# Three attention pairs a cycle instead of two, and a reordered seam inside batch 0, in a fused attention and ReLU-squared kernel

## The chip, the cores and the metric

The program runs on one core of a Trainium2 chip. The metric is device time in microseconds (us) of one execution; lower is better. PE is TensorE, ACT is ScalarE, DVE is VectorE, POOL is GpSimd and SP is SyncE. L286 means line 286 of the kernel before the change.

## The reference

Attention over 8 batches, 12 heads, 448 positions and 64 head dimensions, with one extra term in the softmax denominator, then a two-layer block whose activation is the square of a ReLU:

```
scores = q @ k^T / 8
attn   = exp(scores) / (sum(exp(scores)) + 1)          (written with the maximum taken out)
x      = (attn @ v), heads side by side: 3584 tokens x 768
h      = x @ w_in        (768 x 2048)
out    = relu(h)^2 @ w_out   (2048 x 768), float32
```

Inputs and output are float32; the kernel multiplies in 16 bits and sums in 32.

## The kernel before, in words

**Units.** The work is cut into 54 units in `units`: (batch, pair of heads, first query, number of queries). Batch 0 is done in two query parts, of 192 queries (units 0 to 5) and of 256 (units 6 to 11). From batch 1 on (units 12 to 53) a unit is a pair of heads with all 448 queries. Keys are taken in 4 groups of 112 (`RUN` is 4).

**A unit's steps.** `begin` takes its tiles: `et` for the exponentials (pool of 4), `es` and `half` for their sums. `scores(u, et, c)` (L178) makes half of its scores, c = 0 or 1: two key groups, each in its own PSUM tile `sp`, of which there are two, and ACT takes the exponential of each into `et` (L169). So the second half can only be written where ACT has emptied the first. `add_chunks` (L209) sums the four key groups on DVE in three additions (steps 0, 1, 2; for the short units of batch 0 two, steps 1 and 2), `row_sums` (L239) sums over partitions on PE (L250) and takes the reciprocal on ACT as Ln and Exp (L253, L254): this is Z. `values` (L232) is the product with v on PE (L236), and `normalise` (L257) multiplies by 1/Z on DVE into `xt` (L262 for one unit, L265 for two short ones).

**The two products behind it.** `tile_in` (L290) multiplies xt by w_in, one block of 128 hidden features at a time (two for short parts): 6 steps of two matmuls for a block of 448 tokens, each step half the array wide (L286); DVE then takes the ReLU (L303) and squares it into `gs` (L305). `tile_out` (L320) multiplies gs by w_out for 128 tokens and one half of the 768 columns, in 16 steps. These tasks stand as generators in the lists `ins` and `outs`; `drain(ns)` takes first-product steps up to an amount of time, `run(tiles, n)` whole tasks, `rows(n)` n steps of the second product.

**Modes of PE.** Everything is tiled over halves of PE's array. Scores and `rows` use 64 rows by 128 columns (`ROWS2`: two matmuls side by side into two PSUM tiles, L332, which DVE and ACT add up at L339, L341 and L343). The values, the sums, the transposes and the first product use 128 rows by 64 columns (`COLS2`). At the end, and in `keep_warm` (L427, a product of zeros), the whole array is one piece.

**PSUM.** Two `sp` tiles of two banks each, one bank `xp` and three banks `mp`. From unit 18 on `mp_tile` uses the four single banks in turn.

**Order.** The order is written out by hand, and each engine runs its instructions in that order. Units 0 to 5 (L465) and 6 to 11 (L497) interleave scores, values, transposes of batch 1 and, from unit 7 on, `drain` of the first product for the first 192 tokens. Units 12 to 17 (L536) do the same for batch 1 and drain the rest of that product and the one of the next 256 tokens. Batches 0 to 2 get q and k transposed by PE (`transposes`, L151, at the units of `transpose_at`, L419), later ones by DMA on SP's queue from copies in memory (`stage`, `transposed_loads`). Then 18 cycles (L586) of two units each, three cycles to a batch:

```
scores a, rows(11), scores a, rows(11), scores b, rows(10), scores b      (the stretch in row mode)
values and normalise of the two units before (pending); additions of b    (column mode from here)
pr == 0: rest of ins, queue the first product of batch b-1, one tile_out, loads for batch b+1
early tasks of ins; row_sums of a and b; the other tasks of ins
```

A batch has 16 tasks of `tile_in`, spread 3, 7 and 6 over its three cycles, and 7 halves of `tile_out` on average. After the loop come the last values, three tasks of `tile_out`, and the products of batch 7.

**Loads.** POOL's queue carries, in order, v, the 16-bit q and k of batches 0 to 2 (`load_natural`, tiles `qn` and `kn` in pool `nat`), w_in, w_out and the copies for later batches. A load into a `nat` tile waits until the transposes that read its former contents are done.

Of the kernel before, what the change touches and what calls it, by code (L numbers as in the profile page):

```python
# [15 lines left out]
def kernel(  # L16
# [33 lines left out]
    qk_pool = ctx.enter_context(tc.tile_pool(name="qk", bufs=2))  # L50
    e_pool = ctx.enter_context(tc.tile_pool(name="e", bufs=4))
    es_pool = ctx.enter_context(tc.tile_pool(name="es", bufs=2))
    z_pool = ctx.enter_context(tc.tile_pool(name="z", bufs=2))
    r_pool = ctx.enter_context(tc.tile_pool(name="r", bufs=2))
    osb_pool = ctx.enter_context(tc.tile_pool(name="osb", bufs=2))

# [26 lines left out]
    def load_natural(b, p0, p1):  # L83

        raw = b == 0 and p1 <= 3
        for n, r in (("q", q_r), ("k", k_r)):
            src = r[b, :, 2 * p0:2 * p1]
            if raw:
                if p0 == 0:
                    whole[n] = e_pool.tile([P, RUN * S], FP32, name="et")  # L90
                t = whole[n][:, p0 * 512:(p0 + 1) * 512].rearrange("p (h t d) -> p h t d", h=2, t=RUN)
                (nc.sync if n == "q" else nc.scalar).dma_start(out=t, in_=src)
            else:
                if p0 % 3 == 0:
                    whole[n] = nat.tile([P, NPAIR, RUN, D], FP16, name=f"{n}n{p0 // 3}")
                t = whole[n][:, 2 * (p0 % 3):2 * (p0 % 3 + p1 - p0)]
# [223 lines left out]
    def tile_out(tok, n0, w):  # L320

        if n0 == 0:
            ots[tok] = osb_pool.tile([128, DM], FP32, name="ot")
        ot = ots[tok]
        rows = mode[0] == ROWS2
        op = mp_tile()
        lo = mp_tile() if rows else None
        for fb in range(NFFB):
            g = gs[:, fb, tok % RING:tok % RING + 128]
            if rows:  # L330
                for x, o in ((0, op), (64, lo)):
                    nc.tensor.matmul(o[:, 0:w], g[x:x + 64], wout[x:x + 64, fb, n0:n0 + w],  # L332
                                     start=(fb == 0), stop=(fb == NFFB - 1))
            else:
                product(op[:, 0:w], g, wout[:, fb, n0:n0 + w], start=(fb == 0), stop=(fb == NFFB - 1))
            if fb < NFFB - 1:
                yield w / 2.4
        if rows and n0 == 0:
            nc.vector.tensor_scalar(out=ot[:, n0:n0 + w], in0=op[:, 0:w], scalar1=OUT_SCALE, scalar2=None, op0=ALU.mult)  # L339
        else:  # L340
            nc.scalar.activation(out=ot[:, n0:n0 + w], in_=op[:, 0:w], func=AF.Copy, scale=OUT_SCALE)  # L341
# [52 lines left out]
    def left():  # L394
        return sum(t[0] for t in ins)
# [20 lines left out]
    units += [(b, pr, 0, S) for b in range(1, B) for pr in range(NPAIR)]  # L416
    NU = len(units)

    transpose_at = {pr - 1: (0, pr) for pr in range(1, NPAIR)}  # L419
    for pr in range(NPAIR):  # L420
        transpose_at[NPAIR + 3 + pr] = (1, pr)
    transpose_at[16], transpose_at[17] = (2, 0), (2, 1)

    def keep_warm(n):
        wp = m_psum.tile([128, 512], FP32, name="mp")
# [11 lines left out]
        nc.gpsimd.tensor_copy(last_of, qks[b][0:1, :, 0:1])  # L437

    def begin(i):
        ets[i] = e_pool.tile([P, RUN * 2 * S], FP16, name="et")  # L440
        es = es_pool.tile([P, 2 * S], FP16, name=f"es{i % 2}")
        half = es_pool.tile([P, 1024], FP16, name="half")
        ess[i] = (es, half)
        return units[i], ets[i], es, half
# [20 lines left out]
    for i in range(NPAIR):  # L465
        u, et, es, half = begin(i)
        mode[0] = COLS2
        scores(u, et, 0)
        if i < 2:
            scores(u, et, 1)  # L470
        if i in (3, 5):
            rcp = sums_of(i - 3)
        if i == 0:
            transposes(0, 1, lambda: cast(0, 2, "q"))
            cast(0, 2, "k")
        elif i in transpose_at:
            transposes(*transpose_at[i])
        if i == 0:
            keep_warm(1)
        if i:  # L480
            sums(i - 1)
        if i == 4:
            xp = x_psum.tile([128, 512], FP32, name="xp")
            values_of(2, xp)
        if i > 1:
            scores(u, et, 1)
        if i == 2:
            xp = x_psum.tile([128, 512], FP32, name="xp")
        if i in (2, 3, 4):
            values_of(i - 2 if i < 4 else 3, xp)  # L490
        if i in (3, 5):
            normalise(units[i - 3:i - 1], xp, rcp)
        if i in (1, 3, 5):
            keep_warm(1 + i // 5)


    for i in range(NPAIR, 2 * NPAIR):  # L497
# [4 lines left out]
        mode[0] = COLS2  # L502
        scores(u, et, 0)
        if i == NPAIR:
            values_of(i - 2, xp)
            sums(i - 1)
        if i in transpose_at:
            transposes(*transpose_at[i])
        if i > NPAIR:
            drain(share[0] * 0.45)  # L510
        scores(u, et, 1)
        values_of(i - 1, xp)
        if i == NPAIR:
            keep_warm(2)
        if two:
            rcp = sums_of(i - 2)
        if i > NPAIR:
            drain(share[0] * 0.3)
        else:
            keep_warm(2)  # L520
            normalise(two, xp, rcp)
            queue(0, FIRST)
            share[0] = left() / (NPAIR + 2)
        add_chunks(u, et, es, half, 1)
        if two and i > NPAIR:
            normalise(two, xp, rcp)
# [2 lines left out]
            drain(share[0] * 0.25)  # L529
        if i == NPAIR + 5:  # L530
            load_natural(2, 0, 3)
            for j in range(2):
                load_wout(0, j, 2)


    for i in range(2 * NPAIR, 3 * NPAIR):  # L536
# [4 lines left out]
            xp = x_psum.tile([128, 512], FP32, name="xp")  # L541
        mode[0] = COLS2
        scores(u, et, 0)
        if i in transpose_at:
            transposes(*transpose_at[i])
        if i == 2 * NPAIR + 2:
            load_natural(2, 3, 6)
            for j in range(2):
                load_wout(HALF, j, 2)
            load_v(2, 0, 6)  # L550
            stage(3)
        drain(left() * 0.5 if first else share[0] * 0.45)
        scores(u, et, 1)
        if first:
            done = units[i - 2:i]
# [7 lines left out]
        for step in range(3):  # L563
            add_chunks(u, et, es, half, step)
            drain(share[0] * (0.15, 0.1, 0.15)[step])
        if i == 3 * NPAIR - 1 and ins and ins[0][0] < ins[0][1]:
            run(ins)
        normalise(done, xp, rcp)
        if first:
            queue(FIRST, S - FIRST)  # L570
            share[0] = left() / (NPAIR + 1.5)

# [10 lines left out]
            n -= 1  # L583
        mode[0] = COLS2

    for c in range((NU - 3 * NPAIR) // 2):  # L586
        i = 3 * NPAIR + 2 * c
        b, pr = units[i][0:2]
        new = []
        for j in range(2):  # L590
            new.append(begin(i + j))
        (ua, ea, sa, ha), (ub, eb, sb, hb) = new
        scores(ua, ea, 0)
        rows(11)
        scores(ua, ea, 1)
        add_chunks(ua, ea, sa, ha, 0)
        rows(11)
        scores(ub, eb, 0)
        add_chunks(ua, ea, sa, ha, 1)
        add_chunks(ua, ea, sa, ha, 2)  # L600
        rows(10)
        scores(ub, eb, 1)
        add_chunks(ub, eb, sb, hb, 0)
        mode[0] = COLS2
        for at in pending:
            if at not in rcps:
                rcps[at] = row_sums([units[at]], (ess.pop(at)[0:1],))
            xp = mp_tile()
            values(units[at], ets.pop(at), xp)
            normalise([units[at]], xp, rcps.pop(at))  # L610
        add_chunks(ub, eb, sb, hb, 1)
        add_chunks(ub, eb, sb, hb, 2)
        if b in ON_PE and pr + 2 < NPAIR:
            transposes(b, pr + 2)
            transposes(b, pr + 3)
# [12 lines left out]
        n, early = ((3, 0 if b > 2 else 1), (7, 3), (6, 3))[pr // 2]  # L628
        run(ins, early)
        for at in (i, i + 1):  # L630
            rcps[at] = row_sums([units[at]], (ess.pop(at)[0:1],))
        run(ins, n - early)
        if pr == NPAIR - 2:
            complete(b * S)
        pending = [i, i + 1]
    for at in pending:
        xp = mp_tile()
        values(units[at], ets.pop(at), xp)
        normalise([units[at]], xp, rcps.pop(at))
    mode[0] = FULL  # L640
    run(outs, 3)
    queue((B - 1) * S, S)
# [31 lines left out]
```

## Time and profile before

| | us |
|---|---|
| median of 3 runs | 417.7 (417.44 to 418.12) |
| the profiled execution, its own time | 417.37 |
| its span, first to last instruction | 415.60 |
| PE busy, share of the span | 405.1, 97% |
| DVE busy | 278.0, 67% |
| ACT busy | 238.9, 57% |
| scores of unit 6 / 12 / 18 / 24 begin at | 17.88 / 37.16 / 67.08 / 116.26 |
| one batch of the cycles (batch 4) | 163.75 to 211.25 |

"Busy" counts a matmul from its start to its modelled end, and matmuls overlap, so a busy PE need not be at its peak: whether time is lost is seen from the distances between starts. A timeline line gives start, length, engine, line, operation, result<-inputs, shape and count of merged instructions, and in brackets the idle time before with what ended it. The clock row gives the granted PE clock in tenths; it is full throughout.

### The profile page before, as it was taken

Reading aid. Unit: us, or ns where it says so; the run is one execution under the profiler, and the core shown is the slowest. Engines: PE = TensorE matmul, PEld = TensorE weight load, DVE = VectorE, ACT = ScalarE, POOL = GpSimd, SP = SyncE. Lnnn points to the kernel's source line nnn. Section 1 sums busy time; section 2 is a strip of 40 time slices with the busy share of each in tenths; the row PEclk is TensorE's granted clock in tenths of the full one; section 3 lists DMA queues with packets and bytes.
Section 4 is the critical chain, followed back from the end, with each engine's and each line's share of the span. In section 5 each row is a group of like instructions: output and inputs, shape, how many; then the busy total and the mean of one; then the engine's idle time right before and its main releaser. Section 6 shows DMA issues by size and latency. Waiting matters only on the chain.

```text
span 415.6 us, 10692 instructions
## 1 busy us (share of the span) xinstructions
PE 405.1 (97%) x4719; PEld 256.0 (62%) x4719; DVE 278.0 (67%) x535; ACT 238.9 (57%) x330; POOL 36.4 (9%) x58
## 2 busy tenths in 40 slices
PE   7899999899999999999999999999999999999997
PEld 3567666566566666665666666665666666555664
DVE  4769888778865868568766769659676669287000
ACT  5987998674675664673575564673766655100111
POOL 7523310020000200002000300001000000000000
PEclk9999999999999999999999999999999999999999
DMA  9999999879109960199509871198101101010222
GB/s 202 197 197 198 201 201 219 153 117 207 40 2 196 182 140 2 49 194 185 130 2 171 156 157 35 39 190 151 45 2 39 39 2 39 39 39 0 77 76 77
DMA packets 75823, 45.58 MB, mean 110 GB/s; under 512 B 42560, under 2 KB 72000, under 8 KB 75456
## 3 DMA queue, kind: packets, MB, share of 16 engines
q0 software_dynamic: 28848, 22.16, 35.0%
q1 hardware_dynamic: 46208, 22.05, 23.2%
q8 instruction: 37, 0.61, 0.6%
q10 hardware_dynamic: 720, 0.69, 0.6%
q14 instruction: 10, 0.08, 0.1%
HBM read 45.69 MB, written 17.93 MB: 153 GB/s over the span
## 4 chain that ended last, share of the span: by engine, by line
PE 86%; DMA 8%; ACT 2%; DVE 2%; issue 1%; POOL 0%; POOLq 0%
PE mp L286 23%; PE mp L332 17%; PE mp L288 11%; PE xp L286 8%; PE sp L201 6%; PE xp L332 6%; PE mp L236 5%; DMA kn<-in_k_dram 4%; PE xp L288 3%; DMA win<-in_moe_w_in_dram 3%; PE xp L236 3%; PE sp L189 2%; DMA vn<-in_v_dram 2%; PE mp L250 2%; ACT et L169 1%
## 5 line engine op out<-in xcount | busy, mean ns | idle before, releaser
L169 ACT ACTIVATE et<-sp 112x896 f16<-112x896 f32 (+2 forms) x192 | 165.8, 914 | 53.9 <-PE sp L201 40.2
L286 PEld LDWEIGHTS <-win 128*64 128x64 f16 x1536 | 85.3, 110 | 45.3 <-issue 2.5
L286 PE MATMUL mp<-xt,win 128*64 128x448 f16 (+2 forms) x1236 | 110.2, 324 | 1.2 <-DVE xt L265 0.5
L332 PE MATMUL mp<-wout,gs 64*128 64x384 f16 x864 | 102.3, 322 | 0.0
L332 PEld LDWEIGHTS <-gs 64*128 64x128 f16 x1152 | 56.1, 94 | 31.8
L303 DVE TENSOR_SCALAR rt<-mp 128x448 f16<-128x448 f32 (+2 forms) x99 | 61.5, 621 | 17.2 <-PE mp L286 13.2
L305 DVE TENSOR_TENSOR gs<-rt 128x448 f16<-128x448 f16 (+2 forms) x128 | 50.2, 392 | 4.4
L332 PE MATMUL xp<-wout,gs 64*128 64x384 f16 x288 | 52.6, 323 | 0.0
L253 ACT ACTIVATE rcp<-mp,one_b 128x448 f32<-128x448 f32 (+2 forms) x40 | 25.2, 629 | 40.2 <-PE mp L250 35.9
L214 DVE TENSOR_TENSOR es<-et 112x896 f16<-112x896 f16 x42 | 26.1, 620 | 17.7 <-ACT et L169 17.6
L341 ACT ACTIVATE ot<-mp 128x384 f32<-128x384 f32 (+1 forms) x29 | 14.1, 487 | 36.2 <-PE mp L288 27.6
L201 PE MATMUL sp<-qk 64*112 64x224 f16 x480 | 33.8, 260 | 0.0
L288 PEld LDWEIGHTS <-gs 128*128 128x128 f16 x256 | 24.4, 98 | 15.1 <-issue 0.4
L286 PE MATMUL xp<-xt,win 128*64 128x448 f16 x300 | 32.6, 352 | 0.0
L201 PEld LDWEIGHTS <-qk 64*112 64x112 f16 x480 | 26.3, 128 | 9.7 <-issue 5.4
L236 PEld LDWEIGHTS <-vn 112*64 112x64 f16 x432 | 22.0, 109 | 15.5 <-issue 4.6
L288 PE MATMUL mp<-wout,gs 128*128 128x384 f16 (+1 forms) x192 | 31.0, 322 | 0.0
L343 DVE SCALAR_TENSOR_TENSOR ot<-mp,ot 128x384 f32<-128x384 f32 x27 | 15.1, 558 | 21.7 <-PE sp L201 11.5
L254 ACT ACTIVATE rcp<-rcp 128x448 f32<-128x448 f32 (+2 forms) x48 | 27.7, 577 | 1.5
L216 DVE TENSOR_TENSOR es<-es,half 112x896 f16<-112x896 f16 x42 | 26.2, 625 | 1.4
L189 PE MATMUL sp<-qk 64*112 64x448 f16 (+2 forms) x192 | 24.3, 322 | 2.1 <-ACT et L169 1.3
L214 DVE TENSOR_TENSOR half<-et 112x896 f16<-112x896 f16 x42 | 25.9, 616 | 0.3 <-ACT et L169 0.3
(61 smaller groups left out, 306.6 us busy)
## 6 DMA issues: line engine op xcount, KB each, us to landing
vn<-in_v_dram POOLq DMA_DIRECT2D x7, 672.0 KB, 8.0
out_dram<-ot SPq DMA_DIRECT2D x9, 384.0 KB, 2.3
win<-in_moe_w_in_dram POOLq DMA_DIRECT2D x8, 384.0 KB, 14.0
wout<-in_moe_w_out_dram POOLq DMA_DIRECT2D x4, 768.0 KB, 12.8
stage_q<-in_q_dram POOLq DMA_DIRECT2D x4, 676.0 KB, 10.5
stage_k<-in_k_dram POOLq DMA_DIRECT2D x4, 676.0 KB, 13.6
out_dram<-ot SPq DMA_DIRECT2D x8, 288.0 KB, 2.9
out_dram<-ot SPq DMA_DIRECT2D x9, 192.0 KB, 2.7
```

The costliest lines, as they stand in the source:

```text
L169: nc.scalar.activation(out=out_, in_=in_, func=AF.Exp, scale=scale)
L189: nc.tensor.matmul(sp[:, h, o:o + n], qk[r, 1, x + P * kk:x + P * kk + P], qk[r, 0, x + q0:x + q0 + n], start=True, stop=True)
L201: nc.tensor.matmul(sp[:, odd, h * (S // 2):(h + 1) * (S // 2)], qk[r, which, kx:kx + 2 * P - 1:2], qk[r, 0, x:x + S // 2], start=True, sto ...
L214: nc.vector.tensor_add((es, half[:, 0:2 * S])[step], e[:, 2 * step], e[:, 2 * step + 1])
L216: nc.vector.tensor_add(es, es, half[:, 0:2 * S])
L236: nc.tensor.matmul(xp[64 * h:64 * h + 64, o:o + n], vns[b][:, 2 * pr + h, kk, :], of_head(chunk(et, u, kk // 2, kk), u, h), start=(kk == 0 ...
L254: nc.scalar.activation(out=rcp[:, 0:m], in_=rcp[:, 0:m], func=AF.Exp, scale=-1.0)
L286: nc.tensor.matmul(out_[x:x + 64], lhsT[:, x:x + 64], rhs, start=start, stop=stop)
L288: nc.tensor.matmul(out_, lhsT, rhs, start=start, stop=stop)
L303: nc.vector.tensor_scalar(out=rt[:, 0:m], in0=hp[:, 0:m], scalar1=0.0, scalar2=None, op0=ALU.max)
L305: nc.vector.tensor_mul(gs[:, f0:f0 + per, t0 % RING:t0 % RING + n], r, r)
L332: nc.tensor.matmul(o[:, 0:w], g[x:x + 64], wout[x:x + 64, fb, n0:n0 + w], start=(fb == 0), stop=(fb == NFFB - 1))
```

## The change

**Three units a cycle.** The 36 units of batches 2 to 7 go in 12 cycles of three, two cycles to a batch. Its tasks of `tile_in` are spread 7 and 9. The rows between the six halves of scores are 10, 10, 10, 9 and 9, so a cycle makes three halves of `tile_out` and not two. The last two additions of the third unit stand behind the first tasks of `ins` in the cycle, so that DVE takes the first ReLUs before them; the row sums follow.

**Buffers.** Three units in work and three pending need six tiles for exponentials; `e` has four. The q and k tiles of `nat` become two tiles `nn0` and `nn1`, each of the size of an `et` and holding both q and k, and from unit 22 on every second and third of six units uses them. The pool `z` has three tiles.

**Second product's halves.** In `rows`, the first of the two partial results is scaled into `ot` on DVE for both halves (L339); before, ACT did it for the second half (L341).

**Seam and head.** In unit 4 the values of unit 2 come behind the scores. In unit 6 the additions of unit 5 come first, the values of units 4 and 5 follow one another, their Z and `normalise` come before the second half of the scores, and one of two `keep_warm(2)` goes. In unit 7 the second half of the scores follows the first. The transposes of batch 1 move from units 9 to 14 to units 10, 11, 11, 13, 14 and 15, and those of batch 2 to 16, 17, 17 and, three of them, the first cycle. `drain` takes less in units 7 to 11 and more in 12 to 17, after which all of `ins` is run and Z of unit 17 is made at once. Both halves of w_out are loaded at unit 11, and the second part of q and k of batch 2, its v and the copies of batch 3 at unit 15 instead of 14.

```diff
-    z_pool = ctx.enter_context(tc.tile_pool(name="z", bufs=2))
+    z_pool = ctx.enter_context(tc.tile_pool(name="z", bufs=3))
...
-        if rows and n0 == 0:
+        if rows:
             nc.vector.tensor_scalar(out=ot[:, n0:n0 + w], in0=op[:, 0:w], scalar1=OUT_SCALE, scalar2=None, op0=ALU.mult)
...
-    transpose_at = {pr - 1: (0, pr) for pr in range(1, NPAIR)}
-    for pr in range(NPAIR):
-        transpose_at[NPAIR + 3 + pr] = (1, pr)
-    transpose_at[16], transpose_at[17] = (2, 0), (2, 1)
+    transpose_at = {pr - 1: [(0, pr)] for pr in range(1, NPAIR)}
+    for i, at in ((10, (1, 0)), (11, (1, 1)), (11, (1, 2)), (13, (1, 3)), (14, (1, 4)), (15, (1, 5)), (16, (2, 0)),
+                  (17, (2, 1)), (17, (2, 2))):
+        transpose_at.setdefault(i, []).append(at)
...
     def begin(i):
-        ets[i] = e_pool.tile([P, RUN * 2 * S], FP16, name="et")
+        spare = (i - 3 * NPAIR - 3) % 6
+        if i > 3 * NPAIR + 2 and spare in (1, 2):
+            ets[i] = nat.tile([P, RUN * 2 * S], FP16, name=f"nn{spare - 1}")
+        else:
+            ets[i] = e_pool.tile([P, RUN * 2 * S], FP16, name="et")
...
         if i == NPAIR:
+            sums(i - 1)
             values_of(i - 2, xp)
-            sums(i - 1)
-        if i in transpose_at:
-            transposes(*transpose_at[i])
-        if i > NPAIR:
+            values_of(i - 1, xp)
+            rcp = sums_of(i - 2)
+            normalise(two, xp, rcp)
+            scores(u, et, 1)
+            keep_warm(2)
+            queue(0, FIRST)
+            share[0] = left() / (NPAIR + 4)
+        else:
+            for at in transpose_at.get(i, ()):
+                transposes(*at)
+            if i == NPAIR + 1:
+                scores(u, et, 1)
+                values_of(i - 1, xp)
             drain(share[0] * 0.45)
...
-            share[0] = left() / (NPAIR + 2)
...
-        drain(left() * 0.5 if first else share[0] * 0.45)
+        drain(share[0] * (1.2 if first else 0.45))
...
-        if i == 3 * NPAIR - 1 and ins and ins[0][0] < ins[0][1]:
-            run(ins)
+        if i == 3 * NPAIR - 1:
+            run(ins, len(ins))
+            rcps[i] = row_sums([u], (ess.pop(i)[0:1],))
         normalise(done, xp, rcp)
         if first:
             queue(FIRST, S - FIRST)
-            share[0] = left() / (NPAIR + 1.5)
+            share[0] = left() / (NPAIR - 0.2)
...
+    for i in range(3 * NPAIR, NU, 3):
         b, pr = units[i][0:2]
...
+        for j in range(3):
+            begin(i + j)
+            scores(units[i + j], ets[i + j], 0)
+            if j:
+                add(i + j - 1, 1, 2)
+            rows(10 if j < 2 else 9)
+            scores(units[i + j], ets[i + j], 1)
+            add(i + j, 0)
+            if j < 2:
+                rows(10 if j < 1 else 9)
         mode[0] = COLS2
         for at in pending:
+            take_in(at)
+        if b in ON_PE and pr == 0:
+            for x in range(3):
+                transposes(b, 3 + x)
         if pr == 0:
-            run(ins, len(ins))
             queue((b - 1) * S, S)
             if b > 2:
                 run(outs)
...
+        run(ins, 1 if pr == 0 else 2)
+        add(i + 2, 1)
+        run(ins, 1)
+        add(i + 2, 2)
+        sum_up(i, i + 1)
+        run(ins, 2)
+        sum_up(i + 2)
+        run(ins, 3 if pr == 0 else 4)
+        if pr:
             complete(b * S)
+        pending = [i, i + 1, i + 2]
```

`take_in(at)` is values and normalise of one unit, `add(at, ...)` its additions, `sum_up` its row sums.

More of the change, by code (lines that the diff above doesn't have):

```diff
@@ L93, in load_natural @@
             else:
-                if p0 % 3 == 0:
-                    whole[n] = nat.tile([P, NPAIR, RUN, D], FP16, name=f"{n}n{p0 // 3}")
-                t = whole[n][:, 2 * (p0 % 3):2 * (p0 % 3 + p1 - p0)]
+                if p0 % 3 == 0 and n == "q":
+                    whole["both"] = nat.tile([P, RUN * 2 * S], FP16, name=f"nn{p0 // 3}")
+                w = NPAIR * RUN * D
+                t = whole["both"][:, w * (n == "k"):w * (n == "k") + w].rearrange("p (h t d) -> p h t d", t=RUN, d=D)
+                t = t[:, 2 * (p0 % 3):2 * (p0 % 3 + p1 - p0)]
                 nc.gpsimd.dma_start(out=t, in_=src)
@@ L475 @@
             cast(0, 2, "k")
-        elif i in transpose_at:
-            transposes(*transpose_at[i])
+        else:
+            for at in transpose_at.get(i, ()):
+                transposes(*at)
         if i == 0:
@@ L481 @@
             sums(i - 1)
-        if i == 4:
-            xp = x_psum.tile([128, 512], FP32, name="xp")
-            values_of(2, xp)
         if i > 1:
             scores(u, et, 1)
-        if i == 2:
+        if i in (2, 4):
             xp = x_psum.tile([128, 512], FP32, name="xp")
         if i in (2, 3, 4):
-            values_of(i - 2 if i < 4 else 3, xp)
+            values_of(i - 2, xp)
+        if i == 4:
+            values_of(3, xp)
         if i in (3, 5):
@@ L504 @@
         if i == NPAIR:
+            sums(i - 1)
             values_of(i - 2, xp)
-            sums(i - 1)
-        if i in transpose_at:
-            transposes(*transpose_at[i])
-        if i > NPAIR:
-            drain(share[0] * 0.45)
[L511 to L517, printed above, removed]
-            drain(share[0] * 0.3)
[L519 to L522, printed above, removed]
-            share[0] = left() / (NPAIR + 2)
+            values_of(i - 1, xp)
[5 more added lines that the diff above has]
+            share[0] = left() / (NPAIR + 4)
+        else:
+            for at in transpose_at.get(i, ()):
+                transposes(*at)
+            if i == NPAIR + 1:
+                scores(u, et, 1)
+                values_of(i - 1, xp)
+            drain(share[0] * 0.45)
+            if i > NPAIR + 1:
+                scores(u, et, 1)
+                values_of(i - 1, xp)
+            if two:
+                rcp = sums_of(i - 2)
+            drain(share[0] * 0.3)
         add_chunks(u, et, es, half, 1)
@@ L531 @@
             load_natural(2, 0, 3)
-            for j in range(2):
-                load_wout(0, j, 2)
+            for n0 in (0, HALF):
+                for j in range(2):
+                    load_wout(n0, j, 2)
     for i in range(2 * NPAIR, 3 * NPAIR):
@@ L543 @@
         scores(u, et, 0)
-        if i in transpose_at:
-            transposes(*transpose_at[i])
-        if i == 2 * NPAIR + 2:
+        for at in transpose_at.get(i, ()):
+            transposes(*at)
+        if i == 2 * NPAIR + 3:
             load_natural(2, 3, 6)
-            for j in range(2):
-                load_wout(HALF, j, 2)
             load_v(2, 0, 6)
             stage(3)
-        drain(left() * 0.5 if first else share[0] * 0.45)
+        drain(share[0] * (1.2 if first else 0.45))
         scores(u, et, 1)
@@ L584, in rows, with take_in, add, sum_up @@
         mode[0] = COLS2
-    for c in range((NU - 3 * NPAIR) // 2):
-        i = 3 * NPAIR + 2 * c
-        b, pr = units[i][0:2]
[L589 to L603, printed above, removed]
+    def take_in(at):
+        xp = mp_tile()
+        values(units[at], ets.pop(at), xp)
+        normalise([units[at]], xp, rcps.pop(at))
+    def add(at, *steps):
+        for step in steps:
+            add_chunks(units[at], ets[at], *ess[at], step)
+    def sum_up(*ats):
+        for at in ats:
+            rcps[at] = row_sums([units[at]], (ess.pop(at)[0:1],))
+    for i in range(3 * NPAIR, NU, 3):
+        b, pr = units[i][0:2]
+        for j in range(3):
[8 more added lines that the diff above has]
+                rows(10 if j < 1 else 9)
         mode[0] = COLS2
         for at in pending:
[L606 to L615, printed above, removed]
+            take_in(at)
+        if b in ON_PE and pr == 0:
+            for x in range(3):
+                transposes(b, 3 + x)
         if pr == 0:
-            run(ins, len(ins))
             queue((b - 1) * S, S)
@@ L626 @@
                     stage(b + 2)
[L628 to L633, printed above, removed]
+        run(ins, 1 if pr == 0 else 2)
[7 more added lines that the diff above has]
+        if pr:
             complete(b * S)
-        pending = [i, i + 1]
+        pending = [i, i + 1, i + 2]
     for at in pending:
-        xp = mp_tile()
-        values(units[at], ets.pop(at), xp)
-        normalise([units[at]], xp, rcps.pop(at))
+        take_in(at)
     mode[0] = FULL
```

## The prediction

> **What bounds the kernel.** I read the busy shares, then the stages, then PE's timeline by its starts.
>
> ```profile
> PE 405.1 (97%) x4719; PEld 256.0 (62%) x4719; DVE 278.0 (67%) x535; ACT 238.9 (57%) x330; POOL 36.4 (9%) x58
> 37.20:67.10 29.90, 28.17 (x423) 19.60 (x422) 25.70 (x50) 27.07 (x36) 6.65 (x9) 1.00 1.39 205
> 163.75:211.25 47.50, 47.50 (x575) 30.07 (x574) 34.36 (x66) 29.13 (x40) 2.13 (x4) 1.00 0.62 122
> ```
>
> PE is the bound over the span. From 163.75 to 211.25 (one batch of cycles) it is never idle, but from 37.2 to 67.1 (units 12 to 17) ACT is busy 27.07 of 29.9 us and DVE 25.70. So I price the cycles by what PE does in them, and the head by waits.
>
> In the cycles, distances between starts give prices: a pair of matmuls side by side takes 0.189 us at 448 columns, 0.162 at 384, 0.109 at 256, 0.083 at 192 (24 matmuls of 448 in 2.27 us, for instance); a half of scores 0.385 in row mode. A batch is then 12 halves (4.62), 96 rows (15.58), six units' values at 0.757 (4.54), six row sums (1.14), 16 tasks at 1.136 (18.18) and 16 steps in column mode (2.60): 46.66. It takes 47.49. The 0.83 over falls at the way into and out of row mode, once a cycle:
>
> ```profile
> 161.39 2.44 PE L286 MATMUL mp<-xt,win 128*64 128x448 f16 x24
> 163.75 0.59 PE L201 MATMUL sp<-qk 64*112 64x224 f16 x8
> 164.19 0.32 PE L332 MATMUL mp<-wout,gs 64*128 64x384 f16 x1
> ...
> 168.15 0.55 PE L201 MATMUL sp<-qk 64*112 64x224 f16 x8
> 168.53 1.79 PE L332 MATMUL mp<-wout,gs 64*128 64x384 f16 x20
> 170.15 0.57 PE L201 MATMUL sp<-qk 64*112 64x224 f16 x8
> 170.65 0.95 PE L236 MATMUL mp<-et,vn 112*64 112x448 f16 x8
> 171.43 0.92 PE L236 MATMUL xp<-et,vn 112*64 112x448 f16 x8
> ```
>
> The 24 matmuls last 2.36 to the next start instead of 2.27 (0.09); the first scores last 0.44 and not 0.385 (0.05), the last 0.50 (0.11), the first values 0.78 and not 0.757 (0.02). So 0.278 a cycle (0.83 / 3).
>
> **(a) Three units a cycle: 6 cycles fewer.** 18 ways in and out become 12: 6 x 0.278 = **-1.67 us**. Matmuls of the loop are otherwise as many: 36 x 16 rows either way, tasks 7 + 9 = 3 + 7 + 6.
>
> **(b) Rows of 9.** The second tile of a half needs its PSUM back from the exponential of the half before.
>
> ```profile
> 166.37 1.72 ACT L169 ACTIVATE et<-sp 112x896 f16<-112x896 f32 x2 [0.45 <-PE sp L201]
> 167.98 0.49 ACT L341 ACTIVATE ot<-mp 128x384 f32<-128x384 f32 x1
> 168.54 1.72 ACT L169 ACTIVATE et<-sp 112x896 f16<-112x896 f32 x2
> 170.55 1.72 ACT L169 ACTIVATE et<-sp 112x896 f16<-112x896 f32 x2 [0.28 <-PE sp L201]
> ```
>
> Scores start at 165.97, both exponentials end at 168.09: 2.12 later; PE goes on 0.05 after an exponential that it waited for (ended 44.00, PE at 44.05). So 2.17 after a half starts its successor's second tile may start. It would with 11 rows at 0.385 + 1.785 + 0.19 = 2.36, with 10 at 2.20 (just free, as the trace shows: 168.15 to 170.35), with 9 at 2.04: **0.13 late**. The first 9 waits 0.13; that delays the second half's own tile, so the second 9 just fits. 12 x 0.13 = **+1.6**. ACT's evacuation of 0.49 leaves this stretch and cannot help: the 2.12 holds without it. Bounds: 0 (if some slack is missed) to 24 x 0.13 = +3.2 (both 9s wait).
>
> DVE takes 18 more scalings (12 x 3 / 2) of 0.558 = 10.0 us busy, 288 of some 413. In the stretch it has 7 additions of 0.62 and 3 x 1.17 for the outputs in 10.1 us. PE asks for the third output's first buffer at the third pending unit, 0.50 + 0.78 + 0.76 = 2.0 us after the rows end; DVE frees it about 0.9 after: cover 1.1 us. In the tasks DVE needs 1.01 (0.62 + 0.39) per 1.136 of PE; behind the pending units it starts about 0.9 late and the two additions cost it 1.2 more, but four buffers let it trail by two tasks. I take 0; uncovered, it costs what the rival below says. New `et` buffers have the size of the old: 0, as each was read a cycle earlier (both bounds; a wait would show on ACT).
>
> The Trainium skill, "TensorEngine Tiling (Array Packing)", section Performance Considerations, PSUM Bottleneck, says to share the emptying of PSUM between ScalarE and VectorE, which speaks against moving all scalings to VectorE. By that rule alone the 18 scalings would be a loss, up to the 10.0 us of their busy time; in this trace ACT is the engine that the scores wait for, so I weigh it at 0.
>
> **(c) Head, units 4 to 17.** The waits of PE there:
>
> ```profile
> 19.35 0.52 PE L236 MATMUL xp<-et,vn 112*64 112x192 f16 x8 [1.04 <-DVE xt L265]
> ...
> 23.32 0.36 PE L286 MATMUL mp<-xt,win 128*64 128x192 f16 x4 [0.48 <-DVE xt L265]
> ...
> 44.05 0.40 PE L189 MATMUL sp<-qk 64*112 64x448 f16 x2 [0.44 <-ACT et L169]
> 44.86 0.40 PE L189 MATMUL sp<-qk 64*112 64x448 f16 x2 [0.41 <-ACT et L169]
> ...
> 54.48 0.40 PE L189 MATMUL sp<-qk 64*112 64x448 f16 x2 [0.41 <-ACT et L169]
> ```
>
> Seam, step by step from the timelines: unit 4's second exponential comes 0.7 earlier (PE had it wait behind the values, 16.11), so Ln follows the exponential of unit 5 at 17.2 instead of 17.57, `normalise` ends 0.37 earlier and the values of unit 4 start at about 18.95 for 19.35. Values 4 and 5 (0.33 each), then a wait of 0.4 for the sum of unit 5 (exponential to 19.0, additions 0.96), Z, scores, `keep_warm` (0.43): unit 7 starts at 21.2 for 21.96. Its second half now follows at once and waits for unit 6's exponential, which stands behind Ln and Exp on ACT: to 22.55, a wait of 1.1. Unit 9 waits 0.65 for 1/Z (28.0 to 28.65), since no transposes cover it now. A unit has 11 steps of first product (0.768 us in parts, rounded up) instead of 13. So unit 12 starts at 35.6 for 37.16; 10 steps (0.83) are put off: **-0.7**.
>
> Units 12 to 17: PE's work before is 12 halves at 0.61 (7.34), 5 transposed pairs at 0.39 (1.97), 31 steps of 192 and 84 of 256 (11.7), values 4.2, Z 1.2: 26.4 of 29.9, so 3.5 are waits, nearly all for the exponentials: ACT needs 4.5 a unit (3.3 for four, 1.2 for Ln and Exp), the same as PE's 4.5, and they take turns waiting. The change adds 41 - 31 steps of 192, 96 - 84 of 256, a transposed pair and Z of unit 17: 0.83 + 1.31 + 0.39 + 0.19 = 2.7, all saved elsewhere. PE's unit becomes 4.74 and ACT's wait falls into it: my walk leaves 0.4 in unit 12 and 0.66 in unit 13, so 2.4 less. Against it stands DVE: 25.7 busy plus 0.9, 1.1 and 0.6 is 28.3 of 30.2, 94% in strict order, with additions waiting for exponentials. I give back 1.0 (bounds 0 and all 2.4): **-1.4**.
>
> Loads: POOL's queue keeps its bytes; the four w_out issues (0.91 each) stand together, so the second half of w_out lands near 60 us instead of 64.5, batch 2's second q and k near 65 instead of 57.3 (used after 75), and batch 3's copies at about 74.4 as before: 0. Dropping `keep_warm` could cost PE clock; in this trace the clock stays 1.00 through the 1.04 us gap: 0.
>
> **(d) First cycle.** Before, units 18 and 19 take 15.67 (67.08 to 82.75) for 13.84 of work (the same prices, plus a leftover task of 1.31 and two transposed pairs): 1.83 of waits, of which
>
> ```profile
> 76.33 2.64 PE L286 MATMUL mp<-xt,win 128*64 128x256 f16 x36 [0.46 <-ACT rcp L253]
> 79.32 0.38 PE L250 MATMUL mp<-es,ones 112*64 112x448 f16 x2 [0.36 <-DVE qk L164]
> ```
>
> are the largest: Z of unit 17 made too late, then DVE's pile. Both go. New: Z of unit 17 stands on ACT (1.2 us) just ahead of unit 18's first exponential, and the second half waits for that, 1.0. **-0.8** (bounds -1.8, +0.5).
>
> **Sum.** -1.67 + 1.6 - 0.7 - 1.4 - 0.8 = **-3.0**. The profiled execution took 417.37 (span 415.60, 1.77 around it): 414.4. Its median is 417.7, so **414.7**; about 0.8 us either way (0.2%) is what a measurement tells from no change.
>
> **Rivals.** *Rows of 9 don't wait* ((b) is 0): 413.1. For it: the change takes work off ACT there. Against: 2.12 and 0.05 are steady in every cycle. *The head gives nothing*, DVE or the two new waits (unit 7, unit 18) taking what the old ones gave, so that the change doesn't do what its seam says: (c) and (d) 0, 417.6. For it: DVE at 94%. *DVE's outputs hold up the cycles* (slower): the third output, then an addition, then three `normalise` stand in one queue behind the rows, and the first tasks after them find no free PSUM bank. It decides from 0.25 us a cycle (12 x 0.25 = 3.0); at 0.4, 12 x 0.4 = 4.8, so 419.5. Against: the 1.1 us of cover above.
>
> **Chances.** Forecast (413.4 to 416.2) 0.50, rows free 0.15, head nothing 0.17, slower rival 0.15, anything else 0.03. Faster by over 0.2% takes the first two and 0.07 of the third: 0.72; within 0.2%, 0.10; slower 0.18. Range 412.2 to 418.6: it holds the first three cases and leaves out most of the fourth.
>
> **What would show it.** In a steady batch of the changed kernel: a length of 47.4 to 47.6; one wait of PE L201 for ACT L169 of 0.13 a cycle; no wait of PE L286 or L236 for DVE. In the head: unit 12 at 35.6, unit 18 near 66.8, batch 3 near 112 (0.76 of values deferred in it). I am wrong on (a) and (b) if a batch differs by over 0.3, on (c) if unit 18 comes after 68.5.

## The result and the profile after

The changed kernel takes 416.73 us (median of 4 runs, 416.43 to 416.81) against 417.65 before (median of 4): a ratio of 0.9975, interval 0.9958 to 0.9992, so about 0.9 us faster, where 3.0 were forecast. The profiled execution took 416.75, with a span of 414.98 (before: 417.37 and 415.60). Lines have moved down by two: scores are L191 and L203, exponentials L171, the transposes L158 and their copies L166, values L238, Z L252 to L256, `normalise` L264 and L267, the first product L288, the second L334.

The busy shares, then the windows of units 12 to 17 and of one batch of cycles (columns: busy time and count of PE, PEld, DVE, ACT, POOL, then clock, DMA share, GB/s):

```profile
PE 404.1 (97%) x4717; PEld 271.7 (65%) x4717; DVE 289.8 (70%) x553; ACT 232.9 (56%) x312; POOL 36.7 (9%) x58
```

```profile
36.90:68.80 31.90, 30.56 (x496) 22.60 (x490) 27.82 (x54) 27.49 (x37) 6.30 (x9) 1.00 1.38 206
161.97:209.56 47.59, 47.59 (x574) 32.67 (x572) 36.23 (x69) 28.21 (x37) 2.13 (x4) 1.00 0.62 122
```

A batch takes 47.59, not less than the 47.49 of before: the cycles of three lose what they were built for. In units 12 to 17 DVE is busy 27.82 of 31.9.

Where the 0.62 us between the two spans comes from is read from the starts of scores, with the work that moved between stages set off at the prediction's prices:

| stage | before | after | work moved | difference | forecast |
|---|---|---|---|---|---|
| start to unit 12 | 37.16 | 37.36 | 0.83 put off | +1.0 | -0.7 |
| units 12 to 17 | 29.92 | 31.53 | 2.72 taken on | -1.1 | -1.4 |
| batch 2 | 49.18 | 45.48 | 1.89 done earlier, 0.76 put off | -1.05 | -0.8 |
| batches 3 to 7 | 5 x 47.49 | 5 x 47.60 | none | +0.55 | -0.05 |

The 0.76 put off, the values of one unit, comes after batch 7.

Two rows are off: the head up to unit 12 by 1.7, and the steady batches by 0.6. The waits of PE in the head, and what is around them, from its timeline:

```profile
19.29 0.85 PE L238 MATMUL xp<-et,vn 112*64 112x192 f16 x16 [1.04 <-DVE xt L267]
...
21.48 0.43 PE L191 MATMUL sp<-qk 64*112 64x256 f16 x4
22.79 0.43 PE L191 MATMUL sp<-qk 64*112 64x256 f16 x4 [0.89 <-ACT et L171]
...
29.04 0.63 PE L238 MATMUL xp<-et,vn 112*64 112x256 f16 x8 [0.59 <-DVE xt L267]
...
33.36 0.98 PE L158 MATMUL mp<-ident,nn 112*64 112x112 f16 x32
34.17 0.50 PE L288 MATMUL mp<-xt,win 128*64 128x192 f16 x8
35.75 0.27 PE L288 MATMUL mp<-xt,win 128*64 128x192 f16 x2 [1.08 <-DVE qk L166]
```

The seam has the shape that was walked and comes 0.2 to 0.4 later: the values of unit 4 at 19.29 (forecast 18.95; before 19.35), unit 7 at 21.48 (21.2), its second half at 22.79 (22.55), unit 9's values after their wait for 1/Z at 29.04 (28.65). Some 0.2 of this is a wait for v's load, in PE's weight loads:

```profile
15.95 0.31 PEld L238 LDWEIGHTS <-vn 112*64 112x64 f16 x8 [0.27 <-DMA vn<-in_v_dram]
```

In three of the runs below with the same head (cycles of two, rows of 8, fewer additions) that wait is absent, and unit 7 starts 3.47 to 3.48 after unit 6, for 3.65 here and 4.08 before. Then, in unit 11, stands a wait that the forecast did not have. DVE's timeline shows why:

```profile
34.14 0.69 DVE L267 TENSOR_TENSOR xt<-xp,rcp 128x512 f16<-128x512 f32 x1 [0.55 <-ACT rcp L256]
34.75 0.41 DVE L223 TENSOR_TENSOR es<-half 112x512 f16<-112x512 f16 x1
35.08 1.15 DVE L166 COPY qk<-mp 128x896 f16<-128x896 f16 x2
```

Two transposed pairs, done on PE at 34.17, fill two of the three `mp` banks until DVE copies them out; the third holds the task of the first product that was open. When that task ends after four steps (8 matmuls), the next finds no bank. DVE could not copy, because in its order `normalise` of units 8 and 9 comes first, and that waited for 1/Z from ACT until 34.14. The first copy ran from 35.08, PE went on at 35.75. Four steps from 34.17, at 0.083 each, would have ended at 34.50, so the wait is about 1.2 by the starts.

### The profile page after: what moved, and what is told of

Same layout as the page of the kernel before. It is cut to its first block, busy times and chain, and to the rows that moved or that the text cites. A ratio compares the mean times of both kernels' runs of the same rounds, so it can differ in the third digit from the quotient of the medians.

```text
span 415.0 us, 10686 instructions
## 1 busy us (share of the span) xinstructions
PE 404.1 (97%) x4717; PEld 271.7 (65%) x4717; DVE 289.8 (70%) x553; ACT 232.9 (56%) x312; POOL 36.7 (9%) x58
## 4 chain that ended last, share of the span: by engine, by line
PE 88%; ACT 4%; DVE 3%; DMA 3%; POOL 1%; issue 0%; POOLq 0%
PE mp L288 24%; PE mp L334 17%; PE mp L290 10%; PE xp L288 8%; PE sp L203 6%; PE mp L238 5%; PE xp L334 5%; PE xp L290 3%; PE xp L238 3%; ACT et L171 3%; DMA vn<-in_v_dram 3%; PE sp L191 2%; PE mp L252 2%; ACT rcp L255 1%; POOL nn L99 1%; DVE rt L305 1%
## 5 line engine op out<-in xcount | busy, mean ns | idle before, releaser
L171 ACT ACTIVATE et<-sp 112x896 f16<-112x896 f32 (+2 forms) x144 | 124.2, 913 | 49.8 <-PE sp L203 37.8
L288 PEld LDWEIGHTS <-win 128*64 128x64 f16 x1536 | 85.3, 110 | 45.0 <-issue 2.1
L288 PE MATMUL mp<-xt,win 128*64 128x448 f16 (+2 forms) x1200 | 107.1, 323 | 1.2 <-DVE qk L166 1.2
L334 PE MATMUL mp<-wout,gs 64*128 64x384 f16 x896 | 104.4, 322 | 0.2 <-DVE rt L305 0.2
L334 PEld LDWEIGHTS <-gs 64*128 64x128 f16 x1152 | 69.1, 94 | 19.6 <-issue 0.6
L334 PE MATMUL xp<-wout,gs 64*128 64x384 f16 x256 | 48.0, 322 | 0.0
L171 ACT ACTIVATE nn<-sp 112x896 f16<-112x896 f32 x48 | 41.4, 914 | 6.0 <-PE sp L203 4.3
L343 ACT ACTIVATE ot<-mp 128x384 f32<-128x384 f32 (+1 forms) x16 | 7.6, 477 | 62.1 <-PE mp L290 48.2
L203 PE MATMUL sp<-qk 64*112 64x224 f16 x480 | 36.6, 260 | 0.0
L288 PE MATMUL xp<-xt,win 128*64 128x448 f16 x336 | 36.5, 352 | 0.0
L203 PEld LDWEIGHTS <-qk 64*112 64x112 f16 x480 | 29.6, 127 | 7.4 <-issue 3.6
L238 PEld LDWEIGHTS <-vn 112*64 112x64 f16 x432 | 22.4, 109 | 15.8 <-issue 3.8
L256 ACT ACTIVATE rcp<-rcp 128x448 f32<-128x448 f32 (+2 forms) x48 | 27.7, 577 | 1.5
L216 DVE TENSOR_TENSOR es<-et 112x896 f16<-112x896 f16 x30 | 18.7, 622 | 13.9 <-ACT et L171 13.8
L191 PE MATMUL sp<-qk 64*112 64x448 f16 (+2 forms) x192 | 24.6, 321 | 2.4 <-ACT et L171 1.4
L218 DVE TENSOR_TENSOR es<-es,half 112x896 f16<-112x896 f16 x42 | 26.2, 623 | 0.9
L341 DVE TENSOR_SCALAR ot<-mp 128x384 f32<-128x384 f32 x28 | 15.6, 558 | 14.4 <-PE mp L334 10.9
```

Source lines behind the costliest of these rows:

```text
L171: nc.scalar.activation(out=out_, in_=in_, func=AF.Exp, scale=scale)
L191: nc.tensor.matmul(sp[:, h, o:o + n], qk[r, 1, x + P * kk:x + P * kk + P], qk[r, 0, x + q0:x + q0 + n], start=True, stop=True)
L203: nc.tensor.matmul(sp[:, odd, h * (S // 2):(h + 1) * (S // 2)], qk[r, which, kx:kx + 2 * P - 1:2], qk[r, 0, x:x + S // 2], start=True, sto ...
L218: nc.vector.tensor_add(es, es, half[:, 0:2 * S])
L238: nc.tensor.matmul(xp[64 * h:64 * h + 64, o:o + n], vns[b][:, 2 * pr + h, kk, :], of_head(chunk(et, u, kk // 2, kk), u, h), start=(kk == 0 ...
L256: nc.scalar.activation(out=rcp[:, 0:m], in_=rcp[:, 0:m], func=AF.Exp, scale=-1.0)
```

## The experiments

All ratios are to the kernel before, which ran on the same chip among the runs of each group; its medians there are 417.66 to 417.77, so times of different groups are compared to about 0.1 us.

**The cycles alone**, with units 0 to 17 in the order of before:

```diff
-    (units 0 to 17 of the changed kernel)
+    (units 0 to 17 of the kernel before, all of ins run at the end of unit 17,
+     (2, 2) transposed there too, Z of unit 17 made in the first cycle)
```

> Units 0 to 17 in the order of the kernel before (only all of ins is run at the end of unit 17, and the transposes of the third pair of batch 2 stand there), then the cycles of three. Theory (the cycles lose 0.1 us in each of five batches because the wait for the exponential, measured 0.15 a cycle plus 0.04 at the way out, outweighs the saved way in and out; the gain of the change lies in the first cycle): 417.0 to 418.3, not better than before by more than 0.7. Rival (three units a cycle are where the gain comes from): 416.7 or less.

418.19 (ratio 1.0018, 1.0004 to 1.0032), slower than before. Steady batches take 47.60 here too, so by themselves the cycles of three don't give the 0.9 us. They do give part of batch 2: it goes from 69.20 to 115.34, 46.14, with 1.70 of work done before it and 0.76 put off, so 48.60 against 49.18.

**The head alone**, with the cycles of two:

```diff
-    for i in range(3 * NPAIR, NU, 3):
+    for c in range((NU - 3 * NPAIR) // 2):      (the loop of before; (2, 2) already transposed)
```

> The changed order of units 0 to 17, with Z of unit 17 made there and DVE's scalings, then the 18 cycles of two of the kernel before. Theory: no loss in the steady batches, 47.5 each, and the gain of the first cycle, so 416.0 to 416.7, at or below the changed kernel. Rival (the cycles of three carry the gain): 417.5 to 418.

417.26 (ratio 0.9991, 0.9967 to 1.0016), a miss: not distinguishable from the kernel before, and no better than the change. The steady batches are 47.5 as expected, but batch 2 shows no gain: from unit 18 at 68.66 to unit 24 at 115.86 it takes 47.20, with 1.89 of work already done, so 49.09 against 49.18. So of batch 2's 1.05 in the changed kernel the head alone gives 0.1, the cycles alone 0.6, and the rest comes with both. In the cycle of two DVE still holds up the row sums, here with an addition; PE's timeline:

```profile
79.39 0.38 PE L252 MATMUL mp<-es,ones 112*64 112x448 f16 x2 [0.53 <-DVE es L218]
```

**One transposed pair a unit**:

```diff
-    for i, at in ((10, (1, 0)), (11, (1, 1)), (11, (1, 2)), ...
+    for i, at in ((9, (1, 0)), (10, (1, 1)), (11, (1, 2)), ...
```

> The changed kernel with the transposes of batch 1's first three pairs at units 9, 10 and 11 instead of 10, 11 and 11. Theory (two transposed pairs in one unit fill PSUM while a first-product task is open, so its successor waits 1.08 for DVE's copy; and unit 9's wait of 0.59 for 1/Z would cover 0.39 of transposing): unit 12 starts at about 36.0 instead of 37.36, and 415.0 to 415.8 in all. Rival (DVE has too much to do in the head, and the wait only moves to another unit): 416.4 to 416.9.

415.35 (ratio 0.9948, 0.9935 to 0.9961), as the theory has it. Unit 9's wait, unit 11 and the start of unit 12 in its timeline of PE:

```profile
29.11 0.63 PE L238 MATMUL xp<-et,vn 112*64 112x256 f16 x8 [0.20 <-DVE xt L267]
...
33.62 0.58 PE L158 MATMUL mp<-ident,nn 112*64 112x112 f16 x16
34.04 0.58 PE L288 MATMUL mp<-xt,win 128*64 128x192 f16 x10
34.55 0.42 PE L191 MATMUL sp<-qk 64*112 64x256 f16 x4
...
36.05 0.58 PE L191 MATMUL sp<-qk 64*112 64x448 f16 x4
```

The first product runs through its ten matmuls without a wait, and unit 12 starts at 36.05 (36.0 expected) instead of 37.36. Nothing but the place of two transposed pairs differs, so the wait in unit 11 was theirs. Not all of the gain is that wait: from the start of unit 9 to that of unit 12 it is 1.39 (8.84 for 10.23), of which 0.39 is the pair that unit 9 now takes inside its wait for 1/Z (0.20 left of 0.59), about 1.2 the wait of unit 11, and unit 10 gives back 0.2.

**Rows of 8**, the same 48 rows cut differently:

```diff
-            rows(10 if j < 2 else 9)
+            rows(10 if j < 2 else 8)
...
-                rows(10 if j < 1 else 9)
+                rows(10)
```

> The changed kernel with rows of 10, 10, 10, 10 and 8 between the halves of scores instead of 10, 10, 10, 9 and 9; the work is the same. Theory (the second tile of a half waits until 2.17 after its predecessor's start): the last half waits 0.30 instead of 0.15 for the one before it, 12 x 0.15 = +1.8 us, so 418.3 to 418.8. Rival (the cycles' loss lies elsewhere, in the column stretch or on DVE): 416.5 to 417.0.

418.63 (ratio 1.0020, 1.0010 to 1.0031): 1.9 more than the changed kernel, 1.8 expected. Its batch, in the window from one batch's first scores to the next's:

```profile
162.44:210.37 47.93, 47.67 (x576) 32.28 (x574) 36.41 (x69) 28.17 (x37) 2.13 (x4) 1.00 0.64 121
```

Two cycles cost 0.34 more, 0.17 each (0.15 expected). In the changed kernel the wait is seen in the lengths of the halves of scores and in ACT's line; PE's timeline, then ACT's:

```profile
169.88 0.74 PE L203 MATMUL sp<-qk 64*112 64x224 f16 x8
...
171.88 0.61 PE L203 MATMUL sp<-qk 64*112 64x224 f16 x8
172.41 0.95 PE L238 MATMUL mp<-et,vn 112*64 112x448 f16 x8
```

```profile
166.44 1.72 ACT L171 ACTIVATE et<-sp 112x896 f16<-112x896 f32 x2 [0.30 <-PE sp L203]
168.45 3.58 ACT L171 ACTIVATE et<-sp 112x896 f16<-112x896 f32 x4 [0.29 <-PE sp L203]
172.32 0.92 ACT L171 ACTIVATE et<-sp 112x896 f16<-112x896 f32 x1 [0.29 <-PE sp L203]
```

After a gap of ten rows ACT is idle 0.30 before it gets work; after the first nine it goes on without a break (x4), and PE's half of scores at 169.88 is stretched to 0.74, from 0.56 to 0.60: a wait of 0.15. The last half to the first values takes 0.53 instead of 0.50. So a cycle pays 0.19 for its nines, two cycles 0.38, and saves 0.28 for the third way in and out: +0.10 a batch, which is what the windows show.

**The second halves' scaling back on ACT**:

```diff
-        if rows:
+        if rows and n0 == 0:
```

> The changed kernel with the second half's scaling back on ACT. Theory (ACT is what the scores of a cycle wait for, DVE has time): a scaling of 0.49 stands between two exponentials and makes the next half's second tile 0.12 to 0.15 later, in 12 of the 18 places, so +1.3 to +1.9 and 418.0 to 418.6. Rival (sharing the emptying of PSUM is better): 416.8 or less.

417.84 (ratio 1.0001, 0.9978 to 1.0025): about 1.0 more than the changed kernel, where 1.3 to 1.9 was expected; sharing the emptying of PSUM is not better. In the profile (the batches read have a granted clock of 1.00) batches alternate, 47.87 and 47.59. In those of 47.87, ACT's timeline has the scaling in front of the exponentials that follow a nine:

```profile
125.04 1.72 ACT L171 ACTIVATE et<-sp 112x896 f16<-112x896 f32 x2 [0.28 <-PE sp L203]
126.65 0.49 ACT L343 ACTIVATE ot<-xp 128x384 f32<-128x384 f32 x1
127.02 1.74 ACT L171 ACTIVATE et<-sp 112x896 f16<-112x896 f32 x2
128.91 1.72 ACT L171 ACTIVATE et<-sp 112x896 f16<-112x896 f32 x2 [0.15 <-PE sp L203]
```

In the others a second half ends beside a ten, where ACT has its 0.3 to spare, and costs nothing. The mechanism held; the number of places was 6 in batches 3 to 7 and not 12, at 0.14 each 0.8 of the about 1.0. As to the rule of the Trainium skill cited in the prediction ("TensorEngine Tiling (Array Packing)", PSUM Bottleneck, use both engines): this run speaks against it for a stretch in which the next matmul waits for ScalarE.

**The seam undone** (units 4, 6 and 7 in the order of before, the rest as changed):

```diff
+            values_of(i - 2, xp)
             sums(i - 1)
-            values_of(i - 2, xp)
-            values_of(i - 1, xp)
...
+        scores(u, et, 1)
+        values_of(i - 1, xp)
+        if i == NPAIR:
+            keep_warm(2)
...
-            scores(u, et, 1)
-            keep_warm(2)
```

> The changed kernel with units 4, 6 and 7 in the order of before (two keep_warm, Z of units 4 and 5 behind the second half of the scores, first product between the halves of unit 7); transposes, drains and loads stay. Theory (the seam wins 0.5 by unit 8 and puts off 0.17): +0.2 to +0.5, 416.9 to 417.3. The prediction's price (0.7 with its follow-ups): 417.3 to 417.6. Rival (the new wait of 1.05 for unit 6's exponential eats what the seam gave): 416.4 to 416.8.

417.32 (ratio 0.9982, 0.9961 to 1.0002), 0.6 above the changed kernel by medians, 0.5 set against the kernel before of each group. In its profile unit 12 starts 19.80 after unit 6; in the three runs with the seam and without the wait for v it is 19.36, so 0.44 less (19.53 in the changed kernel's own profile). The seam is worth 0.4 to 0.5: it does what it says, in spite of its new wait.

**First product between the halves of unit 7**, on top of one transposed pair a unit:

```diff
-            if i == NPAIR + 1:
-                scores(u, et, 1)
-                values_of(i - 1, xp)
             drain(share[0] * 0.45)
-            if i > NPAIR + 1:
-                scores(u, et, 1)
-                values_of(i - 1, xp)
+            scores(u, et, 1)
+            values_of(i - 1, xp)
```

> The kernel with one transposed pair a unit (415.35), and in unit 7 the first product's five steps stand between the halves of scores again. Theory (unit 7's wait of 1.05 is for ACT and can hold work): 0.4 less, 414.8 to 415.1. Rival (ACT bounds units 7 to 11, and the wait turns up at unit 9): 415.2 to 415.5.

414.92 (ratio 0.9923, 0.9897 to 0.9948), 0.4 below 415.35, as expected: the wait for unit 6's exponential can hold 0.4 of other work.

**The seventh output half in row mode** in the first cycle of a batch, on top of one transposed pair a unit:

```diff
+        four = pr == 0 and b > 2
...
-            rows(10 if j < 2 else 9)
+            rows(13 if four else 10 if j < 2 else 9)
...
-                rows(10 if j < 1 else 9)
+                rows((13 if j < 1 else 12) if four else 10 if j < 1 else 9)
...
-            if b > 2:
-                run(outs)
...
+        if four:
+            sum_up(i, i + 1)
         run(ins, 1 if pr == 0 else 2)
```

> The kernel with one transposed pair a unit (415.35); in the first cycle of batches 3 to 7 the seventh output half goes in row mode too (rows 13, 13, 13, 12, 13) instead of in column mode behind the values, and the row sums of the first two units stand ahead of the first tasks. Theory (the cycles' loss is the wait behind rows of 9, 0.15 to 0.19 a cycle): 5 x 0.19 = 0.95 less, of which up to 0.5 may go to the first task's wait for the last normalise that the seventh output covered: 414.4 to 414.9. Rival (the cover of that output, or DVE's two more scalings, is worth more than the wait): 415.5 to 417.

414.24 (ratio 0.9917, 0.9890 to 0.9943). Its batch:

```profile
160.37:207.75 47.38, 47.38 (x574) 31.27 (x572) 37.04 (x71) 27.73 (x36) 2.13 (x4) 1.00 0.66 122
```

0.21 less than 47.59 in a batch, one cycle's 0.19, and now below the 47.49 of the kernel before: with gaps of 12 and 13 rows the wait is gone, and the output half was not needed as a cover. The moved row sums are not the cause: in the stretch itself the halves are as far apart as their rows ask (2.49 for 13 rows, 2.34 for 12), which saves 0.15, and the last half to the first values takes 0.48 for 0.53: together the 0.2.

**All three together** (the diffs of the last two, on one transposed pair a unit):

> One transposed pair a unit, first product between the halves of unit 7, and the seventh output half in row mode, together. Theory (three separate waits, so they add up: 1.4 + 0.4 + 1.1 below the changed kernel's 416.7): 413.6 to 414.1. Rival (they share a cause, so that one takes from another): 414.3 or more.

413.75 (ratio 0.9921, 0.9894 to 0.9947): they add up. This is the fastest version, 3.0 below the changed kernel and 3.9 below the kernel before.

**Fewer additions on DVE in units 12 to 16**; the third is left out, so the sums of these units lack half of their terms:

```diff
         for step in range(3):
-            add_chunks(u, et, es, half, step)
+            if step < 2 or i == 3 * NPAIR - 1:
+                add_chunks(u, et, es, half, step)
```

> The changed kernel without the third addition of the exponentials (0.62 on DVE) in units 12 to 16, whose sums thereby lack half of their terms. Theory (DVE is full in units 12 to 17, and the wait of 0.80 for a transposed pair's copy in unit 16 is its backlog): unit 16's wait goes, unit 18 starts 0.7 to 1.0 earlier, 415.7 to 416.1. Rival (ACT bounds these units): 416.4 to 416.8.

415.71 (ratio 0.9954, 0.9942 to 0.9966), 1.0 below the changed kernel. In that kernel, unit 16 has, on PE and then on DVE:

```profile
57.28 1.15 PE L288 MATMUL mp<-xt,win 128*64 128x256 f16 x18
58.36 0.59 PE L191 MATMUL sp<-qk 64*112 64x448 f16 x4
59.58 0.38 PE L252 MATMUL mp<-es,ones 112*64 112x448 f16 x2 [0.63 <-DVE qk L166]
```

```profile
57.84 0.62 DVE L218 TENSOR_TENSOR es<-es,half 112x896 f16<-112x896 f16 x1
58.38 0.62 DVE L264 TENSOR_TENSOR xt<-xp,rcp 128x448 f16<-128x448 f32 x1
58.92 0.61 DVE L166 COPY qk<-mp 128x896 f16<-128x896 f16 x1
```

The pair was transposed before 57.28, but its copy starts at 58.92, behind DVE's queue, and the sum of unit 15 waits for the bank. Without the third addition (L218) PE's timeline has no wait there:

```profile
58.31 0.60 PE L191 MATMUL sp<-qk 64*112 64x448 f16 x4
58.87 0.38 PE L252 MATMUL mp<-es,ones 112*64 112x448 f16 x2
```

Unit 18 starts at 67.84 instead of 68.89. So DVE's backlog was about 1.0 of what units 12 to 17 still lose. It is not all: two waits of PE for exponentials, 0.2 in unit 12 and 0.4 in unit 13, stand in both kernels.

**Cycles of two behind the improved head** (one transposed pair a unit, first product in unit 7):

> The improved head (one transposed pair a unit, first product in unit 7) with the 18 cycles of two. Theory (a steady batch is 0.1 shorter with cycles of two, the first cycles are longer by about 0.7 to 0.9): 415.2 to 415.6 against 414.9 with cycles of three. Rival (cycles of three are better in the steady batches as well): 416 or more.

415.34 (ratio 0.9946, 0.9933 to 0.9959), against 414.92 with cycles of three. Its steady batch is 47.49, as before the change. So cycles of three lose 0.1 in each of five steady batches and win 0.96 in batch 2 (47.20 for 45.48, with 0.76 put off).

## Why the prediction was right in sign and wrong in size

Of the signs that the prediction set, the steady batch held (47.59, for 47.4 to 47.6), and the one against (c) came: unit 18 starts at 68.89, after 68.5.

**(a) Ways in and out of row mode: right.** A batch of the changed kernel is short of one way in and out, 0.28, and the lengths add up with it: 47.49 - 0.28 + 0.38 is 47.59, and with one cycle free of the wait 47.40, for 47.38 measured.

**(b) Rows of 9: right in mechanism, too small.** 0.13 a cycle was forecast for the wait, 0.15 was measured, and the way out after it became 0.03 to 0.04 longer, which the forecast had not priced. 12 x 0.19 is 2.3, not 1.6; -1.67 + 1.6 was to be about nothing and is +0.6. Rows of 8 and of 13 moved it as the theory says, so this is shown. (The upper bound, 24 x 0.13, is 3.1 and not 3.2; it changes nothing.)

**Scalings on DVE: right.** 0 was taken, and putting the 18 back on ACT cost about 1.0. The slower rival's place, the third output's banks, showed no wait of PE.

**(c) Seam: right in kind, somewhat small.** Its own experiment has it at 0.4 to 0.5. Unit 7 was walked to 0.76 earlier than before; it came 0.48 earlier in the changed kernel's profile and about 0.6 in the runs without the wait for v.

**(c) Transposes: the step that failed.** "So unit 12 starts at 35.6 for 37.16; ... -0.7" has no wait for the two transposed pairs that the change puts into unit 11; a pair has only its time on PE (0.39) in the sums. Their copies on DVE (1.15 for two), which stand behind a late `normalise`, and the PSUM banks that they hold until then were left out: 1.08 of idle time, about 1.2 by the starts, which went with one transposed pair a unit. That is most of the 1.76 by which unit 12 starts later than forecast (37.36 for 35.6); 0.4 is the seam, 28.65 to 29.04 at unit 9's values, half of it the wait for v; the last 0.1 to 0.2 was not traced. The rival *the head gives nothing* named DVE for it, by its busy share; DVE is busy 27.82 of 31.9 in units 12 to 17, and what cost the time was the order of its queue.

**(c) Units 12 to 17: nearly right**, -1.1 for -1.4. That DVE would take back about 1.0 of the walk's 2.4 was a guess from its 94%; the run with fewer additions gave back about 1.0.

**(d) First cycle: right in size**, -1.05 with (a) and (b) of that batch for -0.8. (Unit 20's scores begin at 82.84 in the trace, not 82.75, so the waits before were 1.92 and not 1.83.) Z of unit 17 on ACT ahead of the first exponentials costs 0.8 where 1.0 was said: the first two halves of scores stand 2.38 and 2.45 before the next, and 2.05 and 2.00 in the run with the cycles alone, which has that Z later. ACT's timeline of the changed kernel, where unit 18's scores start at 68.89:

```profile
69.00 0.63 ACT L255 ACTIVATE rcp<-mp,one_b 128x448 f32<-128x448 f32 x1 [1.10 <-PE mp L252]
69.67 0.58 ACT L256 ACTIVATE rcp<-rcp 128x448 f32<-128x448 f32 x1
70.15 3.38 ACT L171 ACTIVATE et<-sp 112x896 f16<-112x896 f32 x4
```

The exponentials begin 1.26 after the scores and not 0.44. What was argued wrongly is whose gain it is: not the early Z by itself, since the head alone won 0.1 in batch 2 and the cycles alone, without it, 0.6. How the gain divides between the three copies in one cycle and the additions placed behind the first ReLUs was not tried.

## What to carry to other kernels

When an instruction moves, take along what it holds: a transpose costs its time on PE, but also a PSUM bank from its start to the end of a copy that stands in another engine's queue, and two of them beside an open accumulation stopped PE here for 1.08 us although each is cheap. Fewer and longer cycles save the ways in and out of a mode, but the filler between dependent steps must still be as long as the other engine's answer; compare the gap with it at every place (here 2.17 us against 0.385 + 0.162 a row + 0.19), not on average. Where gaps are too short, put spare work of the same mode into them, as the seventh output half did here, before cutting them evenly.

## What the runs showed that was not expected

The two matmuls of a pair of the second product, side by side on the two row halves, start together only at first. In the changed kernel they start within 0.01 of each other in the first gap, 0.02 to 0.03 apart in the second, 0.03 to 0.04 in the fourth, and 0.05 to 0.06 behind the half of scores that waited:

```profile
162.40 0.32 PE L334 MATMUL mp<-wout,gs 64*128 64x384 f16 x1
162.40 0.32 PE L334 MATMUL xp<-wout,gs 64*128 64x384 f16 x1
...
164.41 0.32 PE L334 MATMUL mp<-wout,gs 64*128 64x384 f16 x1
164.43 0.32 PE L334 MATMUL xp<-wout,gs 64*128 64x384 f16 x1
...
169.72 0.32 PE L334 MATMUL mp<-wout,gs 64*128 64x384 f16 x1
169.76 0.32 PE L334 MATMUL xp<-wout,gs 64*128 64x384 f16 x1
...
171.71 0.32 PE L334 MATMUL mp<-wout,gs 64*128 64x384 f16 x1
171.77 0.32 PE L334 MATMUL xp<-wout,gs 64*128 64x384 f16 x1
```

So it stands already behind gaps of ten, which fit by only 0.03 (2.20 for 2.17); with gaps of 13 and 12 rows the pairs of the first four gaps start within 0.01. The pace stays at 0.16 a row, so it costs nothing by itself. It comes with the longer way out (0.53 for 0.50), and the weight loads of the second product are busy 69.1 us instead of 56.1, as many of them. Why was not tried.
